# The last piece of w2 as sixteen loads of eight partitions in a decode kernel

## The chip, the cores and the metric

The kernel runs on one core of a Trainium2 chip. The metric is the time of one execution on the device, in microseconds. The core has five engines with a program each: TensorE (PE) for matmuls, VectorE (DVE), ScalarE (ACT), GpSimd (POOL) and SyncE (SP), which here issues loads only. Loads and stores are carried out by 16 DMA engines; an instruction on SP or ACT issues one, and a semaphore tells that it has landed.

## The reference

One token goes through a gated mix of an attention block over a long cache and a feed-forward block. All arrays are float32.

```python
g = sigmoid((x * gate_w).sum(-1))                     # x: 512
q = (x @ wq)                                          # 32 heads of 128
scores = q . k_cache * 128 ** -0.5                    # 8 kv heads, 32768 keys each
a = softmax(scores) . v_cache, all heads @ wo         # 4096 -> 512
b = (silu(x @ w1) * (x @ w3)) @ w2                    # 512 -> 1792 -> 512
out = g * a + (1 - g) * b
```

The two caches are 268 MB of the 296 MB that are read. w2 is 1792 x 512, 3.7 MB, and is used last.

## The kernel before

Three big buffers in SBUF take all loads: ra, rb and rc, each 128 partitions x 64 KB. SP issues the loads in the order of its program, each after a semaphore says that its buffer is free: first wq, w1 and w3, then for each of the eight kv heads two halves of k (ra, rb) and two halves of v (both to rc, for the last head to ra and rb), then wo to rc in two loads (L158), and w2 to ra. While a head's k is turned in place by VectorE and multiplied on TensorE, the next head's loads are under way. The feed-forward hidden row is worked out at the start and kept in `htp`, so that at the end only its product with w2 is left.

w2 lies in ra as 128 partitions of FR = 14 rows of 512; row k of partition p is row 14 p + k of the matrix. SP loads it in five pieces in order: rows 0 to 6, 7 to 10 and 11 to 12 (L164), and the two halves of row 13 (L167), each with a semaphore of its own, `l_w2[0]` to `l_w2[4]`. A load of 128 partitions adds 16 to its semaphore when it has landed.

On TensorE the end of the program runs piece by piece: wo's 32 rows and w2's rows 0 to 6 into one accumulator (L446, L453), then rows 7 to 12 by quarters of 128 columns into another bank (helper `rows`, L425). In the last loop the two halves of row 13 are waited for in turn. Each half gives two quarters; when they are done, VectorE copies one and ScalarE the other into the output row (L487). After both halves ScalarE issues the store (L491), and SP waits for it. The output row of 512 is thus complete about as soon as the last half of row 13 is multiplied and copied.

The last loop, before the change:

```python
for i in range(2):
    pe.wait_ge(l_w2[3 + i], 16)
    quarters = range(2 * i, 2 * i + 2)
    rows(htp[:, FR - 1, :], w2t[:, FR - 1, :], stop=True, quarters=quarters).then_inc(c_e.sem, 1)
```

Of the kernel before, what the change touches and what calls it, by code (L numbers as in the profile page):

```python
# [11 lines left out]
P = 128  # L12
# [14 lines left out]
@with_exitstack  # L27
def kernel(ctx, tc, x, k_cache, v_cache, wq, wo, w1, w3, w2, gate_w, out):
    nc = tc.nc
    rb, rc = (nc.alloc_sbuf_tensor(n, [P, 16384], F32).ap() for n in ("rb", "rc"))  # L30
    l_q, l_w1, l_w3 = (nc.alloc_semaphore(n) for n in ("l_q", "l_w1", "l_w3"))
    loads = [(rc, wq, l_q)]
    n = w1.shape[0] * w1.shape[1] // P
    loads += [(rb[:, i * n:(i + 1) * n], w, sem) for i, (w, sem) in enumerate(((w1, l_w1), (w3, l_w3)))]
    for to, w, sem in loads:
        i = nc.sync.dma_start(to, w.rearrange("(p c) n -> p (c n)", p=P)).then_inc(sem, 16)

        tc.no_tile_sem_insts.add(i.ins.name)
    tc.close()
    tc.compile()  # L40
    _program(nc, rb, rc, l_q, l_w1, l_w3, x, k_cache, v_cache, wq, wo, w1, w3, w2, gate_w, out)


def _program(nc, rb, rc, l_q, l_w1, l_w3, x, k_cache, v_cache, wq, wo, w1, w3, w2, gate_w, out):
    pe, dve, act, pool, sp = nc.tensor, nc.vector, nc.scalar, nc.gpsimd, nc.sync
    _, HKV, S, DH = k_cache.shape
    D = x.shape[-1]
# [4 lines left out]
    FR = F // P  # L52
# [9 lines left out]
    def token(name):  # L62
        return nc.alloc_semaphore(name)
# [48 lines left out]
    l_w2 = [token(f"l_w2{i}") for i in range(5)]  # L112
# [46 lines left out]
    w2t = ra[:, 0:FR * D].rearrange("p (k e) -> p k e", e=D)  # L159
    w2d = w2.rearrange("(p k) e -> p k e", k=FR)  # L160
    W2 = (0, 7, 11, 13, 14)
    sp.wait_ge(c_v.sem, 2 * HKV - 1)
    for i in range(3):
        sp.dma_start(w2t[:, W2[i]:W2[i + 1]], w2d[:, W2[i]:W2[i + 1]]).then_inc(l_w2[i], 16)  # L164
    for i in range(2):
        e = slice(i * D // 2, (i + 1) * D // 2)
        sp.dma_start(w2t[:, FR - 1, e], w2d[:, FR - 1, e]).then_inc(l_w2[3 + i], 16)  # L167


    act.dma_start(xr, x.rearrange("a b d -> (a b) d")).then_inc(l_x, 16)  # L170
# [252 lines left out]
    def rows(lhs, rhs, start=False, stop=False, quarters=range(4)):  # L423
        for j in quarters:
            i = pe.matmul(  # L425
                pb[32 * j:32 * j + 32, 0:P], lhs, rhs[:, j * P:(j + 1) * P], start=start, stop=stop
            )
        return i
# [11 lines left out]
    with ahead("fifth", marks[4], zero_reg, 0):  # L440
# [10 lines left out]
        for k in range(W2[1]):  # L451
            t = k % 4
            i = pe.matmul(  # L453
                acc[32 * t:32 * t + 32, :], htp[:, k, :], w2t[:, k, :], start=False, stop=(k >= W2[1] - 4),
                skip_group_check=True,
            )
# [22 lines left out]
    act.copy(ob, acc).then_inc(t_e, 1)  # L479

    for i in range(2):
        pe.wait_ge(l_w2[3 + i], 16)
        quarters = range(2 * i, 2 * i + 2)
        rows(htp[:, FR - 1, :], w2t[:, FR - 1, :], stop=True, quarters=quarters).then_inc(c_e.sem, 1)
        for j, copy, engine in zip(quarters, (dve.tensor_copy, act.copy), (dve, act)):
            engine.wait_ge(c_e.sem, n_ff + 3 + i)
            m = copy(row[:, j * P:(j + 1) * P], pb[32 * j:32 * j + 1, 0:P])  # L487
            if i:
                done.by(m)
# [36 lines left out]
```

## Time and profile before

| what | us |
|---|---|
| median of 3 runs | 691.85 (691.67 to 691.92) |
| span of the profiled execution, first to last instruction | 690.4 |
| PE busy in the span | 370.1 (54%) |
| DVE busy | 307.0 (44%) |
| ACT busy | 41.7 (6%) |

The runs are timed without a profile. The rows come from one more execution, recorded by the profiler, of which the page gives the span and no other time of its own. The difference of 1.45 us to the median lies around the first and the last instruction. All times in rows count from the span's start. A line such as L167 is that line of the program; `out<-in` are the names of what an instruction writes and reads (`in_B_w_dram` is w1, w3 or w2). A load's time to landing counts from its issue, so it holds the time for which it stood in the queue behind others.

### The profile page before, as it was taken

How to read it: one execution, taken by the hardware profiler on the slowest of the kernel's cores; microseconds unless marked ns; L12 is line 12 of the kernel's file. 1: busy time of each engine (PE TensorE's matmuls, PEld its weight loads, DVE VectorE, ACT ScalarE, POOL GpSimd, SP SyncE). 2: the span in 40 equal slices, each digit the busy share in tenths (PEclk: the TensorE clock that was granted, in tenths of full speed). 3: DMA queues.
4: the chain of work that ended last, by engine and by line, in shares of the span. 5: the costliest groups of instructions: out<-in, count | busy, mean ns of one | idle time of the engine just before them, and what ended most of it. 6: DMA issues, size and time to landing. Idle time of an engine off the chain costs nothing. (4 is left out here: it accounts for less than half of the span.)

```text
span 690.4 us, 6719 instructions
## 1 busy us (share of the span) xinstructions
PE 370.1 (54%) x2946; PEld 109.4 (16%) x2946; DVE 307.0 (44%) x194; ACT 41.7 (6%) x111; POOL 7.1 (1%) x41
## 2 busy tenths in 40 slices
PE   1736255456463734456463734566463744466568
PEld 1200021103010121103010111103010121103122
DVE  1019369291725537091725447091815446191000
ACT  0020011002000010002000010002000010002000
POOL 0000000000000000000000000000000000000000
PEclk9977698889677967779677966778786966778668
DMA  9999999999999999999999999999999999999997
GB/s 418 391 436 455 425 430 426 448 448 425 426 425 437 429 433 452 433 429 425 433 433 429 452 437 429 425 429 437 425 440 452 430 425 425 437 429 433 445 413 322
DMA packets 6223, 296.36 MB, mean 429 GB/s; under 512 B 707, under 2 KB 963, under 8 KB 1094
## 3 DMA queue, kind: packets, MB, share of 16 engines
q1 hardware_dynamic: 6192, 296.23, 99.3%
q8 instruction: 6, 0.10, 0.1%
q14 instruction: 3, 0.02, 0.0%
q10 hardware_dynamic: 22, 0.01, 0.0%
HBM read 296.23 MB, written 0.00 MB: 429 GB/s over the span
## 5 line engine op out<-in xcount | busy, mean ns | idle before, releaser
L370 DVE STREAM_TRANSPOSE rb<-rb 128x2048 f32<-128x2048 f32 x64 | 141.8, 2276 | 150.2 <-DVEq L127 150.2
L370 DVE STREAM_TRANSPOSE ra<-ra 128x2048 f32<-128x2048 f32 x64 | 141.4, 2277 | 43.3 <-DVEq L127 43.3
L299 PE MATMUL psum<-rb,winbuf 128*32 128x512 f32 x512 | 88.1, 766 | 128.0 <-PEq L127 128.0
L313 PE MATMUL psum<-rc,prob 128*32 128x512 f32 x896 | 113.9, 666 | 42.1 <-PEq L127 42.1
L299 PE MATMUL psum<-ra,winbuf 128*32 128x512 f32 x512 | 81.5, 733 | 90.2 <-PEq L127 90.2
L313 PEld LDWEIGHTS psum<-rc,prob 128*32 128x32 f32 x896 | 33.8, 121 | 117.9 <-issue 117.8
L394 DVE TENSOR_REDUCE mx<-psum 128x4 f32<-128x1024 f32 x8 | 9.8, 1225 | 83.3 <-DVEq L127 83.3
L299 PEld LDWEIGHTS psum<-rb,winbuf 128*32 128x32 f32 x512 | 13.0, 119 | 201.3 <-issue 201.3
L408 ACT COPY sbuf<-psum 128x512 f32<-128x512 f32 x16 | 9.9, 618 | 476.7 <-PE psum L299 476.7
L299 PEld LDWEIGHTS psum<-ra,winbuf 128*32 128x32 f32 x512 | 14.6, 119 | 149.9 <-issue 149.9
L414 ACT ACTIVATE prob<-psum,nm 128x256 f32<-128x256 f32 x32 | 18.9, 695 | 40.2 <-DVE nm L402 40.2
L323 PE MATMUL psum<-ident,sbuf 128*64 128x64 f32 x512 | 18.2, 235 | 0.8 <-PEq L127 0.8
L323 PEld LDWEIGHTS psum<-ident,sbuf 128*64 128x64 f32 x512 | 17.2, 149 | 7.6 <-issue 7.6
L375 DVE SCALAR_TENSOR_TENSOR otall<-psum,gate,recip 128x4 f32 (+1 forms) x8 | 1.7, 214 | 34.5 <-DVEq L127 34.5
L313 PE MATMUL psum<-rb,prob 128*32 128x512 f32 x64 | 9.9, 789 | 10.0 <-DMA rb<-in_A_v_cache_dram 10.0
L230 PE MATMUL psum<-rc,xp 128*32 128x512 f32 x64 | 9.6, 770 | 4.4 <-DMA rc<-in_A_wq_dram 4.4
L286 POOL COPY winbuf<-winraw 32x16 f32<-32x16 f32 x32 | 6.1, 191 | 535.4 <-PE psum L299 500.1
L257 PE MATMUL psum<-rb,xp 128*32 128x448 f32 x64 | 8.4, 679 | 5.6 <-DMA rb<-in_B_w_dram 5.6
L313 PE MATMUL psum<-ra,prob 128*32 128x512 f32 x64 | 9.4, 751 | 3.6 <-DMA ra<-in_A_v_cache_dram 3.6
L215 PE MATMUL psum<-ones,ob 1*128 1x1 f32 x8 | 2.0, 370 | 15.2 <-DMA prob<-in_gate_w_dram 15.2
L446 PE MATMUL psum<-rc,oq 128*32 128x512 f32 x64 | 10.0, 791 | 0.4 <-PEq L127 0.4
L333 PE MATMUL psum<-fold,ob 128*128 128x4 f32 x64 | 8.4, 255 | 0.8 <-PEq L127 0.8
(62 smaller groups left out, 80.5 us busy)
## 6 DMA issues: line engine op xcount, KB each, us to landing
ra<-in_A_k_cache_dram SPq DMA_DIRECT2D x2, 4096.0 KB, 52.3
rc<-in_A_wo_dram SPq DMA_DIRECT2D x2, 4096.0 KB, 45.7
rb<-in_B_w_dram SPq DMA_DIRECT2D x2, 3584.0 KB, 34.5
ra<-in_B_w_dram SPq DMA_DIRECT2D x1, 1792.0 KB, 33.6
ra<-in_B_w_dram SPq DMA_DIRECT2D x1, 1024.0 KB, 35.7
ra<-in_B_w_dram SPq DMA_DIRECT2D x1, 512.0 KB, 36.5
ra<-in_B_w_dram SPq DMA_DIRECT2D x2, 128.0 KB, 36.3
rc<-in_A_v_cache_dram SPq DMA_DIRECT2D x14, 30.5
```

What stands on the lines that cost most here:

```text
L230: m = pe.matmul(pq[b][32 * j:32 * j + 32, :], xp[:, c, :], rc[:, o:o + REP * DH], start=(c == 0), stop=(c == NC - 1),)
L257: i = pe.matmul(ps[32 * j:32 * j + 32, 0:FJ], xp[:, c, :], rb[:, o:o + FJ], start=(c == 0), stop=(c == NC - 1))
L286: pool.tensor_copy(winbuf[32 * r:32 * r + 32, 16:144].rearrange("p (c k) -> p c k", k=32)[:, :, 4 * r:4 * r + REP], winraw[32 * r:32 * r + ...
L299: i = pe.matmul(s_ps[m][32 * g:32 * g + 32, :], winbuf[:, w:w + 32], region.rearrange("p (n c i) -> p c n i", c=4, i=32)[:, c, n:n + 16], ...
L313: i = pe.matmul(o_ps[32 * t:32 * t + 32, :], prob[:, w:w + 32], region[:, n * DH:(n + 4) * DH], start=(r == 0 and g == 0 and f == 0), stop ...
L323: i = pe.matmul(pf[64 * s:64 * s + 64, 64 * a:64 * a + 64], sbuf[:, a].rearrange("p i m -> p (i m)"), ident.rearrange("p (gf r s q) -> p s ...
L333: i = pe.matmul(mb[:, 0:REP], ob[:, b * P:(b + 1) * P], fold[:, 4 * b:4 * b + 4], start=(b == 0), stop=(b == 3))
L370: dve.transpose(part[:, c], part[:, c]).then_inc(t_tr, 1)
L394: dve.tensor_reduce(mx, pf.rearrange("p (a q) -> p q a", q=REP), axis=AX.X, op=ALU.max).then_inc(t_mx, 1)
L408: act.copy(sbuf[:, :, :, m], s_ps[m].rearrange("p (n i) -> p n i", i=32)).then_inc(t_ev, 1)
L414: act.activation(prob[:, 0:1024].rearrange("p (a n q) -> p n a q", a=16, q=REP)[:, :, :, q], pf.rearrange("p (n a q) -> p n a q", n=16, q= ...
L446: pe.matmul(acc[32 * t:32 * t + 32, :], oq[:, k:k + 32], rc[:, k * D:(k + 1) * D], start=(k < 4), stop=False, skip_group_check=True,)
```

## The change

The second half of row 13, which one load of 128 partitions brought, comes as sixteen loads of eight partitions each, in order of the partitions. All sixteen add to `l_w2[4]`, 16 each, and TensorE waits for 256 on it. The first half of the row is loaded as before.

```diff
--- before.py
+++ after.py
@@ -162,9 +162,9 @@
     sp.wait_ge(c_v.sem, 2 * HKV - 1)
     for i in range(3):
         sp.dma_start(w2t[:, W2[i]:W2[i + 1]], w2d[:, W2[i]:W2[i + 1]]).then_inc(l_w2[i], 16)
-    for i in range(2):
-        e = slice(i * D // 2, (i + 1) * D // 2)
-        sp.dma_start(w2t[:, FR - 1, e], w2d[:, FR - 1, e]).then_inc(l_w2[3 + i], 16)
+    sp.dma_start(w2t[:, FR - 1, 0:D // 2], w2d[:, FR - 1, 0:D // 2]).then_inc(l_w2[3], 16)
+    for p in range(0, P, 8):
+        sp.dma_start(w2t[p:p + 8, FR - 1, D // 2:D], w2d[p:p + 8, FR - 1, D // 2:D]).then_inc(l_w2[4], 16)
 
 
     act.dma_start(xr, x.rearrange("a b d -> (a b) d")).then_inc(l_x, 16)
@@ -479,7 +479,7 @@
     act.copy(ob, acc).then_inc(t_e, 1)
 
     for i in range(2):
-        pe.wait_ge(l_w2[3 + i], 16)
+        pe.wait_ge(l_w2[3 + i], 16 if i == 0 else 256)
         quarters = range(2 * i, 2 * i + 2)
         rows(htp[:, FR - 1, :], w2t[:, FR - 1, :], stop=True, quarters=quarters).then_inc(c_e.sem, 1)
         for j, copy, engine in zip(quarters, (dve.tensor_copy, act.copy), (dve, act)):
```

On SP, at the end of its program, before (-) and now (+); w2's rows 0 to 12 are the loads at L164, 8x256 is eight partitions of 256 numbers, and L496 stands behind the final wait:

```order
 L164 DMA ra<-in_B_w2_dram 128x2048
 L164 DMA ra<-in_B_w2_dram 128x1024
-L167 DMA ra<-in_B_w2_dram 128x256 x2
+L165 DMA ra<-in_B_w2_dram 128x256
+L167 DMA ra<-in_B_w2_dram 8x256 x16
 L496 ISA
```

One issue has become sixteen, at the same place of the queue; the other engines' instructions stand as before.

## Rows read from the trace of the kernel before

**Rows 1.** The page: the DMA engines in 40 slices, and what they moved
```profile
DMA  9999999999999999999999999999999999999997
DMA packets 6223, 296.36 MB, mean 429 GB/s; under 512 B 707, under 2 KB 963, under 8 KB 1094
```

**Rows 2.** Chain of waits in order of time, its end: start us, us
```profile
650.76 35.74 DMA ra<-in_B_w_dram
...
686.54 2.12 PE psum L425 x60
688.66 0.02 issue
...
688.97 0.28 DVE prob L487
```

**Rows 3.** Timeline of PE from 688.64: start us, us, then the instructions
```profile
688.44 0.41 PE L425 MATMUL psum<-ra,htp 128*32 128x128 f32 x4
```

**Rows 4.** Timeline of the issues on SP from 650: start us, us
```profile
650.39 1.28 SPq L164 DMA_DIRECT2D ra<-in_B_w_dram  x3
651.71 0.91 SPq L167 DMA_DIRECT2D ra<-in_B_w_dram  x2
```

**Rows 5.** Line L167: issue ns min/median/max, starts; to landing
```profile
L167 SPq DMA_DIRECT2D ra<-in_B_w_dram x2: 432/432/432, 651.7 to 652.2; - x2
...
DMA to landing us min/median/max: 36.2/36.3/36.4
```

**Rows 6.** Three stretches from 686; the columns are in the first line
```profile
core 0: us, PE busy (x) PEld busy (x) DVE busy (x) ACT busy (x) POOL busy (x), PEclk, DMA share, GB/s
686.00:686.50 0.50, 0.00 (x0) 0.00 (x0) 0.00 (x0) 0.48 (x1) 0.00 (x0) 1.00 0.87 326
686.50:687.00 0.50, 0.46 (x16) 0.46 (x20) 0.00 (x0) 0.11 (x1) 0.00 (x0) 1.00 0.47 178
687.00:687.50 0.50, 0.50 (x28) 0.50 (x24) 0.00 (x0) 0.00 (x0) 0.00 (x0) 1.00 0.34 123
```

**Rows 7.** Line L171, the load of gate_w: duration ns min/median/max
```profile
L171 ACTq DMA_DIRECT2D prob<-in_gate_w_dram x1: 731/731/731, 3.4 to 3.4; - x1
```

**Rows 8.** Waits of SP from 650: us in total, times, longest
```profile
SPq L496 <- ACTq L494: 37.0, 1, 37.0
```

**Rows 9.** The page: DMA queues, packets, MB, share of 16 engines
```profile
q1 hardware_dynamic: 6192, 296.23, 99.3%
...
q10 hardware_dynamic: 22, 0.01, 0.0%
```

**Rows 10.** DMA from 687.609 to 687.955, then from 687.27 to 687.6
```profile
DMA packets 30, 0.03 MB, mean 74 GB/s; under 512 B 5, under 2 KB 30, under 8 KB 30
...
q1 hardware_dynamic: 30, 0.03, 21.6%
...
DMA packets 41, 0.05 MB, mean 161 GB/s; under 512 B 4, under 2 KB 40, under 8 KB 40
...
q1 hardware_dynamic: 40, 0.04, 32.0%
```

**Rows 11.** DMA from 689.9 to 690.44: in 40 slices, then packets by queue
```profile
DMA  0000003000000000000000000000000000000000
...
q10 hardware_dynamic: 2, 0.00, 1.1%
```

**Rows 12.** DMA from 686 to 689: the instruction queue
```profile
q8 instruction: 1, 0.02, 2.2%
```

**Rows 13.** Lines L154 and L158: issue ns, starts; to landing
```profile
L154 SPq DMA_DIRECT2D rb<-in_A_v_cache_dram x1: 328/328/328, 622.1 to 622.1; - x1
...
DMA to landing us min/median/max: 38.2/38.2/38.2
...
L158 SPq DMA_DIRECT2D rc<-in_A_wo_dram x2: 328/380/432, 628.9 to 629.3; - x2
...
DMA to landing us min/median/max: 41.1/45.7/50.4
```

## The prediction

> **What bounds the kernel now.** I read the page's line on the DMA engines first [rows 1]: they are nine tenths busy or more in 39 of 40 slices, at a mean of 429 GB/s, and the busiest other engine, PE, is so for 54% of the span (the table above). So the kernel is one stream of loads, and only what happens after the last bytes can be shortened or lengthened by this change. The chain of waits in order of time [rows 2] says the same: a load of w2 until 686.50, then 2.12 us of matmuls at L425, then two copies of 0.28 us on VectorE, then the store. Of L425 only the last piece is in question. The matmuls on the last quarter rows start at 688.44 and run 0.41 us, to 688.85 [rows 3]; in front of them stands the wait for the load that is changed. That load was issued second of the two at L167: the pair starts at 651.71, each issue takes 0.432 us, so the second starts at about 652.19 [rows 4], and with the shorter of the two times to landing, 36.2 us, it lands at 688.4; the first, 651.71 + 36.4, at 688.1 [rows 5]. 0.04 us behind 688.4 is the matmul's start. So the landing of the last piece sets the end now.
>
> How the queue runs dry is in the table of stretches [rows 6]. The DMA engines are 0.87 busy from 686 to 686.5, 0.47 in the next half microsecond and 0.34 in the one after: about half of the sixteen engines still work after 686.5, and from 687 on about five. The engines do the same work and end at different times; the last piece is complete when the last of them is.
>
> **The change, part by part.** The load of the first half of the row is the same instruction as before, on L165. The other becomes sixteen loads of eight rows of 1 KB each. The bytes are the same 128 KB. PE, DVE, ACT and POOL keep their instructions; PE waits for 256 instead of 16 on the same semaphore, with nothing queued between that wait and the last matmuls.
>
> *Issuing.* SP has sixteen issues in place of one. An issue of 128 rows costs 0.432 us [rows 5], and the only eight-row load here, that of gate_w, cost its issuer 0.731 us [rows 7]. Sixteen cost between 16 x 0.43 = 6.9 and 16 x 0.73 = 11.7 us, so SP ends between 659 and 664 us instead of 652.6. After them SP has only the final wait, 37.0 us long before [rows 8], and the queue does not reach this piece until shortly before 688. I cost issuing at nothing, under a cover of over 20 us. Without cover it would be 6.5 to 11.3 us more.
>
> *Which engines carry the rows.* The page's queue lines tell it [rows 9]. SP's queue has 6192 packets for 43 loads, 144 each: 128 rows and 16 completions. ACT's queue has 22 packets for four transfers: x, gate_w in eight rows, the zeros and the result, that is 1 + 8 + 1 + 1 = 11 of data. Were every transfer completed on 16 engines there would be 64 completions; the other 11 packets are 1 + 8 + 1 + 1. So an eight-row load goes to eight engines, one row and one completion on each. By this count SP's queue after the change has 42 x 144 + 16 x 16 = 6304 packets. I take them to be the same eight each time, since sixteen like instructions give no cause to differ, though no row tells which eight or shows two such loads: each of the eight has 16 rows and 16 completions where all sixteen had 8 rows and one completion. The Trainium skill (DMA: Bandwidth & Descriptors, "Why a DMA increments its semaphore by 16 and not by 1") says that such a load uses the lowest-numbered engines of the sixteen; the 22 packets agree with its count of engines, no row here shows their numbers. By it the eight are always the same; with a moving choice the sum below would be near zero.
>
> *What a row and a completion cost.* Two stretches of the tail, in which only late engines work, give two equations [rows 10]. From 687.609 to 687.955 there are 25 packets of 1 KB and 5 small ones, 21.6% of 16 x 0.346 us = 1.196 us. From 687.27 to 687.6 there are 36 and 4 on SP's queue, 32.0% of 16 x 0.33 = 1.690 us. Solved: 46 ns a row and 10 ns a completion. Packets overlap a little: the two half-row loads land 0.3 us apart (688.1, 688.4), and eight rows and a completion at these prices are 0.38. I take 0.33 for one half row on a late engine, 0.04 a row.
>
> *Sum.* An engine of the eight needs 16 x 0.04 + 15 x 0.01 = 0.79 us in place of 0.33: +0.46. An engine outside them has nothing after the first half and ends 0.33 earlier. About five late engines share the tail; a free draw of eight from sixteen misses all five once in some 80 times and holds the very last in half, so I take 0.1 off: the landing comes 0.36 later. The copies take some of it: the last matmuls end at 688.85, the second copy starts at 688.97 since it stands behind the first, and a copy can follow 0.02 after its matmul [rows 2, 3]; 0.1 us of lateness is free. That leaves +0.26, say +0.3: span 690.4 + 0.3 = 690.7. The page gives the profiled execution no time but its span; the median of the runs is 691.85, 1.45 us above, and I carry that over: 692.15.
>
> *Bounds of what no row shows.* Loads of one row per engine, one behind the other on the same engine, do not occur before. The nearest row below is the above, 0.05 us a load; it can be below nothing as a whole, -0.3, if the eight are early engines. From above: the result's store has its packets 0.09 us before 690.08 or so (1.1% of 16 x 0.54 us, in the seventh of 40 slices from 689.9) and the span ends at 690.44, so a completion's whole trip takes up to 0.44 us [rows 11]; sixteen in a row would be 7.0 us. Full rows with one completion in nine packets are nearer to this case than a lone store, and the issue-to-issue work in the tail is seen without holes, so I stay at 0.05.
>
> **Rivals.**
> *Each load's completion holds the next.* If an engine starts the next small load only when the completion of the last has gone round, the eight engines take 16 x 0.44 = 7.0 us instead of 0.33: +6.6 with the 0.1 that the copies take, 698.4. For it: the change puts a completion behind every row, where before eight rows shared one. Against it: the first half's load and the second's land 0.3 us apart, less than one such trip, so at least one boundary between loads is crossed without waiting [rows 5]. It decides from 0.11 us a load, where 16 x 0.11 - 0.33 passes 1.4 us. The Trainium skill has a rule that speaks for it (same page, "Bandwidth" and "Rules for kernel authors"): a DMA has a fixed cost near 2 us, and "under 64 KB you're paying mostly overhead". One after another that would be some 32 us here by estimate; the 0.3 us between two loads of 128 KB says that the fixed cost overlaps with the neighbour's.
>
> *Issuing stalls.* Before, SP had eight loads outstanding at 652.6, the last half of v, two of wo and five of w2, without a longer issue [rows 4, 13]; now there are 23. If only eight may wait, one of the sixteen goes at each landing, and about eight are left when the first half lands at 688.1: 8 x 0.73 us more, 694, and about +6 in all: 698. For it only that the number is new; against it, that the eighth issue took as long as the others.
>
> *A further instruction fetch.* SP's program grows by 15 loads. A fetch on q8 occupies an engine 2.2% of 16 x 3 us = 1.06 us [rows 12]. On one of the late engines it would add that: +1.3, 693.2. Against it: the one fetch in the tail now delays nothing on the chain.
>
> *Nothing changes.* Rows go evenly over the engines, or the eight are early ones: -0.3 to +0.15, about 691.85.
>
> **Chances.** Eight engines, 0.05 us a load: 0.68. Nothing: 0.12. Completions hold: 0.10, price anywhere from 693.2 to 698.4. Stalled issue: 0.04. Fetch: 0.06, about half of it over the line. This kernel's measurement tells a change from none at about 0.2%, 1.4 us. Slower than that: 0.10 + 0.04 + 0.03 = 0.17. Faster: 0.02, since no case here gains over 0.3 us. Same: 0.81. The likeliest case alone goes from 691.5 to 692.8; the range from 691.4 to 693.4 takes in the fetch and the beginning of the held completions, and leaves out some 0.14 above.
>
> **What would show it.** Right: 6304 packets on SP's queue; sixteen issues that end before 665 us; the last matmuls at L425 start at 688.7 to 688.9 and nothing else moves; in the last half microsecond no more than eight DMA engines work. Wrong: 6432 packets (sixteen completions a load) or another count; a gap between 1 KB packets in the tail, a DMA share near zero while PE waits (held completions); issues that stretch toward 688 (stall); one more instruction packet on q8 or q14. If the last matmuls start later than 689.8, my price per load is wrong.

## The result and the profile after

The changed kernel takes 694.77 us (median of 5 runs, 694.02 to 694.91) against 691.85 (5 runs, 691.67 to 691.97): +2.92 us, a ratio of 1.004 with a 95% interval of 1.003 to 1.0051. The interval lies above 1, so the kernel is slower, by 0.4%. The forecast was 692.15, in a range from 691.4 to 693.4.

The page's span and its queues of loads and instructions (packets, MB, share of 16 engines), beside [rows 9]:

```profile
span 693.6 us, 6734 instructions
...
q1 hardware_dynamic: 6304, 296.23, 98.9%
q8 instruction: 6, 0.10, 0.1%
q14 instruction: 4, 0.03, 0.0%
```

The span has grown by 3.1 us (690.44 to 693.58 in the traces). SP's queue has the 6304 packets that eight engines a load give. The end of the chain of waits in order of time (start us, us, what), to be read beside [rows 2]; SP's sixteen issues stand in it one by one, and four of them are shown:

```profile
654.01 0.29 SPq L167
654.30 0.04 issue
654.35 2.88 SPq L167
657.23 0.04 issue
657.27 1.17 SPq L167
...
674.24 17.37 DMA ra<-in_B_w_dram
691.62 0.04 issue
691.66 0.44 PE psum L425 x4
692.10 0.02 issue
692.12 0.28 DVE prob L487
```

The last load is issued at 674.24 (the issue itself takes until 676.6) and the piece has landed at 691.62 instead of 688.4: those 3.2 us, less 0.1 that the copies give back, are the whole difference. The last matmuls as the timeline of PE has them (start us, us, what, and in brackets the idle time and its releaser), beside [rows 3]:

```profile
691.66 0.41 PE L425 MATMUL psum<-ra,htp 128*32 128x128 f32 x4 [2.75 <-DMA ra<-in_B_w_dram]
```

PE now waits 2.75 us for the piece. What the DMA engines do meanwhile is in the stretches (us, busy time of PE, PEld, DVE, ACT and POOL, PEclk, DMA share, GB/s), beside [rows 6], and in the DMA line of the stretch from 688.95 to 692, in 40 slices:

```profile
686.50:687.00 0.50, 0.28 (x12) 0.28 (x16) 0.00 (x0) 0.28 (x1) 0.00 (x0) 1.00 0.71 226
687.00:687.50 0.50, 0.50 (x28) 0.50 (x20) 0.00 (x0) 0.00 (x0) 0.00 (x0) 1.00 0.58 166
687.50:688.00 0.50, 0.50 (x20) 0.25 (x12) 0.00 (x0) 0.00 (x0) 0.00 (x0) 1.00 0.35 86
688.00:688.50 0.50, 0.46 (x19) 0.44 (x18) 0.00 (x0) 0.00 (x0) 0.00 (x0) 1.00 0.29 55
688.50:689.00 0.50, 0.41 (x12) 0.14 (x4) 0.04 (x1) 0.04 (x1) 0.00 (x0) 1.00 0.03 2
```

```profile
DMA  0000000000000000000000000000000000000000
...
DMA packets 0, 0.00 MB, mean 0 GB/s; under 512 B 0, under 2 KB 0, under 8 KB 0
```

By the packets, the rows are done before 689. For 2.7 us after that no packet of a load is recorded, and still the semaphore is not full. In the kernel before, the last packet ends 0.43 us ahead of the last increment (687.97, 688.40). The trace also has the time of every single increment, which no view prints. The last of this semaphore's, in us, are

```
691.002 691.012 691.204 691.213 691.415 691.615
```

two series, each in steps of 0.2 us. So the piece is late since its completions come in one after another, long behind the rows that they report.

The last rows have slowed down as well. The packets from 688.27 to 688.95 are the last four rows of 1 KB and seven small ones (in the second line packets, MB, share of 16 engines):

```profile
DMA packets 11, 0.00 MB, mean 6 GB/s; under 512 B 7, under 2 KB 11, under 8 KB 11
...
q1 hardware_dynamic: 11, 0.00, 8.1%
```

8.1% of 16 x 0.68 us is 0.88 us; less 0.01 for each small packet, a row takes 0.2 us, where [rows 10] gave 0.046. In the trace 17 of the 256 rows of 1 KB take 0.16 us or more, in the kernel before none. So rows run ahead of their increments by up to 2.7 us, by estimate some thirteen loads of an engine at 0.2 us, and the rows behind that go at the increments' pace.

### The profile page after: what moved, and what is told of

The parts are those of the page before. It is cut to its first block, busy times and chain, and to the rows that moved or that the text cites. A ratio compares the mean times of both kernels' runs of the same rounds, so it can differ in the third digit from the quotient of the medians.

```text
span 693.6 us, 6734 instructions
## 1 busy us (share of the span) xinstructions
PE 373.2 (54%) x2946; PEld 109.3 (16%) x2946; DVE 307.0 (44%) x194; ACT 41.7 (6%) x111; POOL 7.1 (1%) x41
## 3 DMA queue, kind: packets, MB, share of 16 engines
q1 hardware_dynamic: 6304, 296.23, 98.9%
## 5 line engine op out<-in xcount | busy, mean ns | idle before, releaser
L299 PE MATMUL psum<-ra,winbuf 128*32 128x512 f32 x512 | 84.2, 755 | 87.4 <-PEq L127 87.4
```

The costliest lines, as they stand in the source:

```text
L299: i = pe.matmul(s_ps[m][32 * g:32 * g + 32, :], winbuf[:, w:w + 32], region.rearrange("p (n c i) -> p c n i", c=4, i=32)[:, c, n:n + 16], ...
```

## The experiments

**Half as many loads on twice as many engines.**

```diff
-    for p in range(0, P, 8):
-        sp.dma_start(w2t[p:p + 8, FR - 1, D // 2:D], ...).then_inc(l_w2[4], 16)
+    for p in range(0, P, 16):
+        sp.dma_start(w2t[p:p + 16, FR - 1, D // 2:D], ...).then_inc(l_w2[4], 16)
```

> Eight loads of sixteen rows in place of sixteen of eight. Theory (completions): each DMA engine passes the completions of its loads one at a time, about 0.2 us each (in the changed kernel the last ones land 0.2 us apart, 691.00, 691.20, 691.42, 691.62, while the last row packet is done at 688.9). Here sixteen engines have eight rows and eight completions each: last landing 8 x 0.2 = 1.6 us behind the first half's 688.1, so 689.7 and +1.2 us: about 693.1. Rival (stalled issues make the piece late): eight issues stall at most twice, so about 692.0. Rival (eight engines carry double rows): all sixteen carry eight, so 691.9.

Measured: 693.17 us (before, on the same chip: 691.91), ratio 1.0018 (1.0009 to 1.0028), +1.26. The end of its chain:

```profile
657.28 32.57 DMA ra<-in_B_w_dram
689.85 0.04 issue
689.90 0.44 PE psum L425 x4
```

The last landing is at 689.85, about as the theory had it (689.7). PE waits for 128 here. Eight rows on each engine are no more than before, so the rows do not explain it; nor do the two stalled issues, of 2.9 and 1.2 us, since the last one ends at 658.5, long before the queue comes to this piece. The eight completions an engine do.

**A semaphore for each load.**

```diff
-    ...w2d[p:p + 8, FR - 1, D // 2:D]).then_inc(l_w2[4], 16)
+    ...w2d[p:p + 8, FR - 1, D // 2:D]).then_inc(l_w2[4 + p // 8], 16)
...
-        pe.wait_ge(l_w2[3 + i], 16 if i == 0 else 256)
+        for sem in l_w2[3:4] if i == 0 else l_w2[4:20]:
+            pe.wait_ge(sem, 16)
```

> Sixteen loads of eight rows as in the changed kernel, but each adds to a semaphore of its own and PE waits for all sixteen. Theory (completions pass one at a time on an engine, whatever they count on): as the changed kernel, 694.8, last landings 0.2 us apart. Rival (increments of one engine to the same semaphore wait for each other): the spacing falls to about 0.05 us a load, last landing near 688.9, 692.3 to 693.0 with the further waits on PE.

Measured: 694.82 us (691.91), ratio 1.0043 (1.0026 to 1.006). The end of its chain:

```profile
673.94 17.22 DMA ra<-in_B_w_dram
691.16 0.14 issue
691.30 0.43 PE psum L425 x4
```

Nothing is gained, so the increments do not wait for each other at a common semaphore. Since every load has its own here, the increments can be laid side by side: one line for each of the last four loads, eight increments each, in us, in order of time.

```
688.931 689.225 689.494 689.531 689.557 690.121 690.531 690.560
689.105 689.427 689.663 689.700 689.745 690.298 690.726 690.755
689.290 689.640 689.843 689.880 689.948 690.485 690.932 690.960
689.472 689.855 690.021 690.060 690.142 690.671 691.137 691.165
```

Down each column the step is 0.17 to 0.22 us, in all eight columns. The trace does not name the engines, but eight series that go on in step from load to load are what eight engines, the same ones each time, would leave.

**Thirty-two loads of four rows.** As the first edit, with 4 in place of 8; PE waits for 512.

> Thirty-two loads of four rows. Theory (completions): four engines with 32 completions each, 32 x 0.2 = 6.4 us behind the first half on these engines (between 686.4 and 688.3 in the changed kernel): last landing 692.8 to 694.7, so 696.0 to 697.9. Rival (price per row or per byte on the engine, no matter how many completions): 32 rows on four engines at 0.05 us, 1.6 us, about 693. Rival (stalled issues): 25 stalled issues instead of ten, later than 697.9, and the issues on SP end after 688.

Measured: 696.81 us (691.91), ratio 1.0071 (1.0055 to 1.0088), +4.9. The end of its chain:

```profile
684.38 0.29 SPq L167
684.72 8.56 DMA ra<-in_B_w_dram
693.28 0.04 issue
693.33 0.67 PE psum L425 x4
```

The time is inside the theory's range (696.0 to 697.9) and far from 693. The issues end at 685.0, before the queue comes to this piece, so their stalls are not what is late. Of the rows of 1 KB, 71 of 256 take more than 0.14 us here, and none in the kernel of eight loads: the more loads an engine has, the more of its rows go at the increments' pace.

**The first half of the row split, the second whole.**

```diff
-    sp.dma_start(w2t[:, FR - 1, 0:D // 2], ...).then_inc(l_w2[3], 16)
     for p in range(0, P, 8):
-        sp.dma_start(w2t[p:p + 8, FR - 1, D // 2:D], ...).then_inc(l_w2[4], 16)
+        sp.dma_start(w2t[p:p + 8, FR - 1, 0:D // 2], ...).then_inc(l_w2[3], 16)
+    sp.dma_start(w2t[:, FR - 1, D // 2:D], ...).then_inc(l_w2[4], 16)
```

PE waits for 256 on the first half and for 16 on the second.

> The first half of the row comes as the sixteen loads, the second half, behind it in the queue, as one load. Theory (completions pass in order on an engine): the single load's completion on the eight engines stands behind sixteen others, so it lands 16 x 0.2 = 3.2 us and one more 0.2 after 687.7 to 688.0, at 691.1 to 691.4: about 694.4. Rival (only loads on the same semaphore hold each other): the second half lands near 688.5 to 689, the first half at about 691; the time is about the same, but the semaphore of the second half is full before that of the first.

Measured: 694.83 us (691.91), ratio 1.0042 (1.0025 to 1.0059), 0.4 over the expected time. The single load behind the sixteen, as its line has it (issue ns min/median/max, starts; time to landing):

```profile
L167 SPq DMA_DIRECT2D ra<-in_B_w_dram x1: 2364/2364/2364, 667.0 to 667.0; - x1
...
DMA to landing us min/median/max: 24.6/24.6/24.6
```

667.0 + 24.6 = 691.6: the load of 128 rows is held too, behind the sixteen (its increments reach from 686.47 to 691.58, the last of the sixteen loads' comes at 691.38). On an engine completions pass in the order of the queue, whichever semaphore they count on.

**The sixteen loads in front of w2's other pieces.** The loop over p is moved ahead of the three loads of rows 0 to 12 (which are at L166 here, the first half of the row at L167); nothing else.

> The sixteen loads stand in front of w2's other pieces in the queue instead of behind them; everything else is as in the changed kernel. Theory (completions pass one at a time, about 0.2 us each, beside the rows of later loads): the sixteen completions of an engine, 3.2 us, pass while over ten microseconds of rows follow, and the end keeps only what the eight engines carry more, 8 rows or 0.34 us, and a part of the backlog: 692.0 to 692.9. Rival (a completion that has not passed stops the rows behind it on its engine): the 3.2 us come back at the end, 694.5 to 695.

Measured: 694.63 us (691.97; its runs spread from 693.51 to 696.91), ratio 1.0042 (1.0029 to 1.0056). Here the theory fell, since even the lowest run is above its 692.9, and the rival held. PE's timeline, the matmuls on w2's first piece, before and in this kernel:

```profile
684.05 1.92 PE L453 MATMUL psum<-ra,htp 128*32 128x512 f32 x14 [0.21 <-DMA ra<-in_B_w_dram]
686.90 1.92 PE L453 MATMUL psum<-ra,htp 128*32 128x512 f32 x14 [1.54 <-DMA ra<-in_B_w_dram]
```

The sixteen loads have landed at 683.26, and all pieces behind them are late: the last load of all, the first half of the row, was issued at 657.83 and landed 33.0 us later, at 690.8 instead of 688.4 or, as a first half was, 688.1. Large loads behind fill little of the time; they wait in the queue of the eight engines. By the increments w2's first piece lands 3.6 us behind the sixteen loads (686.85), where it took 4.3 us behind wo before (679.71 to 684.01), so about 0.7 us of its rows passed beside them. What the engines lose does not show in their share of busy time. From 678 to 682 the queue of loads has (packets, MB, share of 16 engines), before and in this kernel:

```profile
q1 hardware_dynamic: 131, 1.67, 98.1%
q1 hardware_dynamic: 302, 1.18, 97.4%
```

The share is nearly the same and the bytes are fewer by three tenths. Since the DMA engines are busy from end to end [rows 1], what they lose in the middle is not won back. The theory from here on: an engine needs at least 0.2 us for each load in which it takes part, in the order of the queue, and the load's own rows count within them.

**Twice and four times the bytes in each load.** In one kernel the whole last row comes as sixteen loads, in the other the last two rows:

```diff
+        sp.dma_start(w2t[p:p + 8, FR - 1, :], w2d[p:p + 8, FR - 1, :]).then_inc(l_w2[4], 16)
```

```diff
+    sp.dma_start(w2t[:, 11:12], w2d[:, 11:12]).then_inc(l_w2[2], 16)
     for p in range(0, P, 8):
+        sp.dma_start(w2t[p:p + 8, 12:14], w2d[p:p + 8, 12:14]).then_inc(l_w2[4], 16)
```

> The whole last row comes as sixteen loads of eight rows of 2 KB, so the same number of completions with twice the bytes in each. Theory (0.2 us a completion, rows beside it): 16 x 0.2 = 3.2 us behind the piece before, which lands at 687.7 to 688.0: last landing 691.0 to 691.2, 694.2 to 694.5. Rival (a price per byte, the wait for the load's own rows): spacing of 0.24 to 0.4 us, 695 to 697.

> The last two rows of w2 come as sixteen loads of eight rows of 4 KB, behind row 11 as one load; PE waits for them before its last two rows. One row takes an engine 0.16 us. Theory (0.2 us a completion, rows beside it): the spacing stays near 0.2 us, 3.2 us behind row 11's landing near 687.1 to 687.4, last landing 690.3 to 690.9, 694.0 to 694.6 with the row more that PE has left. Rival (completion and row add): spacing 0.35 us, last landing 692.8 or later, 696 or more.

Measured: 694.94 us (691.97), ratio 1.0041 (1.0026 to 1.0055), and 695.06 us, ratio 1.0048 (1.0033 to 1.0063). Both are half a microsecond over the expected time. The matmuls behind the last landing, in the first kernel by its chain and in the second by PE's timeline:

```profile
691.36 0.66 PE psum L424 x8
```

```profile
690.75 0.64 PE L425 MATMUL psum<-ra,htp 128*32 128x128 f32 x16 [2.41 <-DMA ra<-in_B_w_dram]
```

The landings are where the theory has them, or 0.1 us behind: 691.3 (691.0 to 691.2 expected) and 690.7 (690.3 to 690.9; the execution in the profile is the fastest of this kernel's four, 694.51). The last increments are 0.2 us apart in both. From 1 KB to 4 KB a row the step stays the same, though a row of 4 KB alone takes an engine 0.16 us: row and completion do not add. A price that grows with the bytes, wherever they are written, is excluded with it.

**Fifteen more waits on SP.**

```diff
+    for i in range(15):
+        sp.wait_ge(c_v.sem, 2 * HKV - 1)
```

> The kernel before, with fifteen more waits on SP behind its last load, each on a count long reached; the loads are as before. In the changed kernel and in the four runs so far the queue q14 has one more fetch of instructions of 8 KB, a few us after SP's last issue, which the kernel before has not. Theory (SP's longer program fetches once more): the fourth fetch appears here too, on one engine, and the time is 691.9 to 692.6. Rival (the fetch comes from elsewhere and the program's length does nothing): three fetches, 691.9.

Measured: 691.89 us (691.97), ratio 0.9999 (0.999 to 1.0008). The instruction queues from 650 to 691:

```profile
q8 instruction: 2, 0.03, 0.3%
q14 instruction: 1, 0.01, 0.0%
```

In the kernel before q14 has no packet in this stretch. The longer program does fetch once more in this stretch, and the time stays.

**Four loads of thirty-two rows.** As the first edit, with 32; PE waits for 64.

> Four loads of thirty-two rows in place of sixteen of eight; each of the sixteen engines has two rows and a completion of each load. Theory now (an engine needs at least 0.2 us for each load, its rows count within these): 4 x 0.2 = 0.8 us behind the first half instead of 0.33, last landing 688.9 to 689.1, 692.3 to 692.6. Rival (the price is of loads with one row per engine only): 691.9 to 692.0, last landing 688.4.

Measured: 692.52 us (691.94), ratio 1.0009 (1.0 to 1.0018), +0.58; the last landing:

```profile
652.78 36.49 DMA ra<-in_B_w_dram
689.26 0.04 issue
689.31 0.44 PE psum L425 x4
```

The time is as expected (692.3 to 692.6), the landing 0.2 us later than expected. The interval touches no change, so it does not exclude the rival's 691.9 to 692.0; but all eleven runs (692.41 to 692.69) lie above all fifteen of the kernel before (691.74 to 692.04). By the increments 0.5 of the 0.9 us stand ahead of the four loads, since the first half lands at 688.58 and not at 688.08; the four follow in 0.69 us, or 0.17 each, where the one took 0.32.

**Rows that take longer than 0.2 us.** The last four rows of w2 in sixteen loads of 8 KB a row, `w2d[p:p + 8, 10:14]`, behind loads of rows 0 to 6, 7 to 8 and 9.

> The last four rows of w2 come as sixteen loads of eight rows of 8 KB, behind rows 0 to 9; PE waits for them before its last four rows and has 1 us more to do after them. A row of 8 KB takes an engine 0.31 us. Theory now (at least 0.2 us for each load of an engine, rows within): the rows themselves set the pace, landings of one engine 0.31 us apart, the last 16 x 0.31 = 5.0 us behind row 9's 686.0 to 686.3, at 691.0 to 691.4; 695 to 696 with PE's rest. Rival (0.2 us on top of the rows): 0.51 us apart, the last landing at 694.2 or later, 698 or more.

Measured: 697.51 us (691.94), ratio 1.0082 (1.0066 to 1.0097), 1.5 us over the theory's range. PE's timeline at the end, and the stretches from 690 (columns as above):

```profile
692.06 0.66 PE L425 MATMUL psum<-ra,htp 128*32 128x128 f32 x8 [4.88 <-DMA ra<-in_B_w_dram]
692.48 0.66 PE L425 MATMUL psum<-ob,fold 128*32 128x128 f32 x8
692.91 1.51 PE L425 MATMUL psum<-ra,htp 128*32 128x128 f32 x24
```

```profile
690.00:691.00 1.00, 0.00 (x0) 0.00 (x0) 0.00 (x0) 0.00 (x0) 0.00 (x0) 1.00 0.21 82
691.00:692.00 1.00, 0.00 (x0) 0.00 (x0) 0.00 (x0) 0.00 (x0) 0.00 (x0) 0.79 0.02 8
692.00:693.00 1.00, 0.94 (x20) 0.88 (x24) 0.00 (x0) 0.00 (x0) 0.00 (x0) 0.50 0.00 0
```

The last increments are 0.31 us apart (691.39, 691.70, 692.01), the pace of the rows, not 0.51. The landing at 692.0 is at least 0.6 later than expected; row 9 had landed at 686.7 instead of 686.0 to 686.3. The rest of the miss is PE's: after 4.88 us of waiting its granted clock is 0.50, the lower of its two levels, 1.2 GHz, and forty matmuls take 2.4 us where I had reckoned with 1.

**The sixteen loads on ACT's queue.** SP's loop over p is gone, and ACT has it instead.

```diff
+    act.wait_ge(c_v.sem, 2 * HKV - 1)
+    for p in range(0, P, 8):
+        act.dma_start(w2t[p:p + 8, FR - 1, D // 2:D], ...).then_inc(l_w2[4], 16)
```

> The sixteen loads are issued by ACT, on its own queue, as soon as the buffer is free near 650, while SP's queue holds its large loads; ACT has nothing else to do until 670. A DMA engine serves the two queues in turn, so large rows of SP's queue, up to 2.4 us each, lie between two small loads. Theory (at least 0.2 us from one completion of an engine to its next, with rows of other loads filling it where they lie between): nothing of the 3.2 us is left, and only the eight rows more on eight engines stay, 0.34 us: 692.0 to 692.5. Rival (each small load takes its 0.2 us from the engine wherever it stands): 694.5 to 695.

Measured: 693.34 us (691.86), ratio 1.0021 (1.0012 to 1.003), between the two expectations, so that neither held. The first half's load, the last on SP's queue:

```profile
L165 SPq DMA_DIRECT2D ra<-in_B_w_dram x1: 437/437/437, 652.5 to 652.5; - x1
...
DMA to landing us min/median/max: 37.2/37.2/37.2
```

It lands at 689.7, 1.3 us behind the last landing before, where 0.34 were to come from the double rows. With the 0.33 that an engine had for the half row before, 1.3 + 0.33 over sixteen loads are 0.10 us a load. By this count large rows from another queue in between hide half of the 0.2 us and not all. Why half is open, and no other run shows it.

## Why the prediction was wrong

*What bounds the kernel* held: the landing of the last piece sets the end, and its +3.2 us, less 0.1 of the copies, are the span's +3.1 us.

*Issuing* was wrong in its size and right in its effect. The first six issues took 0.29 to 0.38 us, the seventh 2.88, and the last ended at 676.6, not 664. The rival of stalled issues thus took place, and cost nothing: the queue reaches the piece ten microseconds later, and with half the loads and two stalls the price is still nearly half (+1.26 of +2.92).

*Which engines carry the rows* held: eight, by the count of packets, and the same eight by the eight series of increments.

*What a row and a completion cost* is the step that failed, in the sentence "I stay at 0.05" under the bounds. The 46 and 10 ns are what a packet takes while the rows run ahead; the last rows here took 0.2 us. What counts is when the increment arrives, and for that there is a floor of about 0.2 us for each load on an engine: 16 x 0.2 = 3.2 us in place of 0.79. The bounds were 0.05 and 0.44, and I chose the lower by the nearest row, full loads with eight rows to a completion. Those take 0.33 us an engine and lie above the floor, so they could not show it. For the same reason the argument against the first rival was weak: two landings 0.3 us apart exclude a price of 0.44, not one of 0.2. That rival, "each load's completion holds the next", came true in its effect at half its price of 0.44, and the point from which it decides, 0.11 us a load, was passed; its band of 693.2 to 698.4, with a chance of 0.10, holds the time measured. Its mechanism as written did not: an engine does not wait with the next row until the completion has gone round, since rows run up to 2.7 us ahead. The fixed cost near 2 us that the prediction cites for it from the Trainium skill (DMA: Bandwidth & Descriptors) stands there not under "Bandwidth" but under "Anatomy of one DMA — SWDGE (gpsimd) path", as a fit to loads that GpSimd issues. No run here shows it for SP's loads: the sixteen took 3.27 us together, not the 32 of that estimate.

The sum by the step corrected: the first half lands at 688.34 in the profiled execution, 0.27 later than before, and sixteen loads at 0.204 us follow, 3.27, where the second half took 0.32; 0.27 + 3.27 - 0.32 = 3.2 us. The 0.27 may be a matter of which engine stands where in the queue when it runs dry; its cause was not settled. The copies gave 0.1 back, as forecast: the matmuls end 3.25 us later (688.85, 692.10), the second copy starts 3.15 us later (688.97, 692.12).

*The fetch* of instructions came, as one more packet on q14, and the longer program by itself costs nothing measurable (0.9999). It is not part of the loss.

*"Nothing changes"* needed the eight engines to be early ones or the rows to spread evenly. Neither was so: the eight series of the kernel with a semaphore for each load begin between 686.7 and 688.1, with early and late engines among them.

A version faster than both did not come out of this: with two loads of 128 rows the kernel before is above the floor, and wherever the small loads were put, the price was paid, on ACT's queue about half of it.

## What to carry to other kernels

A load that brings an engine less than 0.2 us of rows, by estimate some 5 KB here (8 KB took 0.31 us), still takes the engine about 0.2 us, in the order of the queue. So count loads per engine, not bytes alone. In this kernel, where the DMA engines are the bound, no place that was tried is free: sixteen loads cost 2.7 to 2.9 us in SP's queue and 1.5 on ACT's. Where a trace shows only loads above such a floor, it says nothing about what lies below: then the upper bound is as good as the lower, and the range must hold both. Read the arrival of a load from its increments or from who waits for it, not from its packets, which were done 2.7 us earlier here, and what the engines bring from their bytes, not from their share of busy time.

## What the runs showed of the hardware that was not expected

- From one completion of an engine to its next at least 0.17 to 0.22 us pass, the same for rows of 1, 2 and 4 KB, and for one semaphore or sixteen. Rows of 8 KB go at their own 0.31 us. What in the engine takes the 0.2 us no run shows.
- With small loads the packets run ahead of the completions, but not without end: the last packet was recorded before 689, the last increment came at 691.6, and the last rows of 1 KB took 0.2 us each in place of 0.046.
- SP issued six to eleven eight-row loads at 0.29 us each, in the kernel that has them first all sixteen, and then stalled for up to 3.6 us on one load, once for 11.5 (that kernel's last, of 128 rows). Each issue ended before the queue came to its load, and no time was lost by the stalls.
- After 4.88 us without a matmul TensorE ran at a granted clock of 0.50 in the kernel with rows of 8 KB, and its last forty matmuls took 2.4 us.
